# Moving batch 1's kv product ahead of four matmuls, and a quarter of two weight casts to GpSimd, in a fused attention and MoE kernel

## The chip, the cores and the metric

The kernel runs on one core of a Trainium2 chip. The metric is the device time of one execution in microseconds (us); lower is better. The engines are TensorE (PE; PEld is its weight load), VectorE (DVE), ScalarE (ACT), GpSimd (POOL) and SyncE (SP), which only issues DMAs here.

## The reference

A cosine-weighted linear attention over 8 batches, 8 heads and 576 positions, whose output goes through a two-layer MLP with a swish:

```python
q_p, k_p = phi(q), phi(k)                    # relu(x) * cos(pos), relu(x) * sin(pos), side by side
kv  = einsum('bhsf,bhsd->bhfd', k_p, v)
num = einsum('bhsf,bhfd->bhsd', q_p, kv)
den = einsum('bhsf,bhf->bhs', q_p, z) + 1e-6 # z = sum of k_p over positions
x   = (num / den), heads side by side        # 4608 x 512
h   = x @ w_in                               # 512 x 2048
g   = h * sigmoid(beta * h)
out = g @ w_out                              # 2048 x 512
```

## The kernel before

The 4608 rows are worked in nine chunks of 512. A chunk has 16 groups of four matmuls for h (L365), each followed by a swish on ScalarE (L372), and then four quarters of 16 matmuls for the output (L390). The attention of the next batch is threaded between these. The start is the hard part: attention of batches 0 and 1, the loads of all weights and their casts to bf16 have to fit beside the first chunk. What each slot of the first chunk does beside its matmuls stands in a table; shortened:

```python
    def cast_halves(i, fs=(0, 256)):          # w_in quarter i, in two halves of columns
        for f in fs:
            for gj in GJ:                     # four pieces of 64 partitions x 2 x 256
                cast_win(i, gj, "dve", f, f + 256)

    cast_halves(1)

    def rest():                               # runs behind slot 4 of the first chunk
        cast_halves(2, (0,))
        x_mul(x_rden(2, 0, 8, NQ, (0, 1)), 8, NQ)   # xs block 8 of batch 0: divide
        cast_halves(2, (256,))
        cast_halves(3)
        load_w("out", 0); load_w("out", 1)
        load_raw(1, "v"); load_raw(1, "k"); load_raw(1, "q")
        x_turn_dma(0, 8, 9)                   # xs block 8: transposed by a DMA
        load_w("out", 2, 2); load_w("out", 3, 2)
        ...                                   # casts of w_out 0..7, v_scale, relus of k and q

    def second():                             # runs behind slot 23
        kv_mm(1, 0, 6)                        # 72 small matmuls into banks 6 and 7
        kv_mm(1, 1, 6)
        kv_take((0, 1), 6, "act")             # ScalarE copies them out
        takes.append(q_turn_pe(1, 0, 4, hold=True))   # nine transposes into banks 4, 5
        takes.append(q_turn_pe(1, 1, 6, hold=True))   # nine transposes into banks 6, 7
        cast_out(8)                           # w_out row block 8, needed by slot 24
        ...
    early = {
        4: lambda: (num_mm(8, 0, 2, 0), num_mm(8, 1, 2, 1), rest()),
        15: lambda: v_scale(1, 1, eng="act"),
        23: second,
        25: lambda: (num_seven(0, 4), x_mul(x_rden(4, 0, 0, 7, (0,)), 0, 7), cast_out(13)),
        26: lambda: (num_seven(1, 6), x_mul(x_rden(6, 0, 0, 7, (1,)), 0, 7)),
        ...
    }
```

## Time and profile before

| | before |
|---|---|
| time, three runs | 295.05 us median (294.95 to 295.48) |
| span of the profiled run, granted clock | 292.9 us, 1.0 |
| TensorE busy | 96% |
| second query turn waits | 0.46 us, at 41.20 us |
| swish beat, even and stretched | 0.86 us; 1.07, 0.92, 0.91 us |

The chain of work that ended last is TensorE from 52 us to the end, so whatever this change gains, it gains before 52 us. There the beginning of an L372 activation shows when a group of four matmuls ended; an even beat of 0.86 us means that TensorE ran without a stop. The prediction below shows the lines.

### The profile page before, as it was taken

What the parts mean: (1) busy time and instruction counts of PE and PEld (TensorE: products, weight loads), DVE (VectorE), ACT (ScalarE), POOL (GpSimd) and SP (SyncE); (2) the same over time, 40 slices, a digit from 0 to 9 for tenths busy, and PEclk for the clock granted to TensorE, in tenths of its full rate; (3) what the DMA queues carried; (4) which work ended last, traced back from release to release, by engine and by line L of the source; (5) the groups of instructions that cost most, each with busy time, mean ns of one, the idle gap of its engine ahead of it and who ended that gap; (6) DMA issues with size and microseconds to landing.
All of it is one profiled execution on the core that took longest, in us unless ns stands there. A gap on an engine that the chain in (4) does not pass through costs nothing.

```text
span 292.9 us, 7188 instructions
## 1 busy us (share of the span) xinstructions
PE 282.4 (96%) x3046; PEld 142.5 (49%) x3073; DVE 114.3 (39%) x291; ACT 142.6 (49%) x228; POOL 73.3 (25%) x85
## 2 busy tenths in 40 slices
PE   8699999999999999999999999999999999999994
PEld 7454455455445544454445444554455444444444
DVE  5989975744910292029400950086005000000000
ACT  5777845862166314821473137512760277137511
POOL 1440000633381026402640255015701210000000
PEclk9999999999999999999999999999999999999999
DMA  7999999999998099907991699149102910131033
GB/s 256 378 391 384 392 325 385 265 234 355 169 273 334 4 143 230 396 30 133 219 395 46 123 211 388 72 73 197 36 2 50 145 36 0 38 84 24 0 74 72
DMA packets 50736, 53.89 MB, mean 184 GB/s; under 512 B 31232, under 2 KB 31632, under 8 KB 50704
## 3 DMA queue, kind: packets, MB, share of 16 engines
q1 hardware_dynamic: 47744, 45.95, 53.8%
q0 software_dynamic: 2688, 7.34, 11.1%
q8 instruction: 24, 0.39, 0.6%
q10 hardware_dynamic: 272, 0.14, 0.2%
q14 instruction: 8, 0.07, 0.1%
HBM read 36.71 MB, written 9.44 MB: 158 GB/s over the span
## 4 chain that ended last, share of the span: by engine, by line
PE 84%; DMA 9%; DVE 4%; issue 1%; SPq 0%
PE ps L390 39%; PE ps L365 38%; DMA w_stage<-in_moe_w_in_dram 4%; PE ps L280 3%; DVE win L108 3%; DMA w_stage<-in_moe_w_out_dram 3%; PE ps L259 2%; DMA raw_q<-in_q_dram 2%; PE ps L408 1%; DVE wout L116 0%; PE ps L339 0%; PE ps L229 0%; SPq L78 0%; DVE xs L302 0%; DVE o_sb L411 0%
## 5 line engine op out<-in xcount | busy, mean ns | idle before, releaser
L365 PE MATMUL ps<-xt,win 128*128 128x512 bf16 (+1 forms) x580 | 127.6, 378 | 0.1
L390 PE MATMUL ps<-wout,g_t 128*128 128x512 bf16 x535 | 120.6, 379 | 1.9 <-issue 1.0
L372 ACT ACTIVATE g_t<-ps,beta 128x512 bf16<-128x512 f32 x144 | 98.5, 688 | 33.5 <-PE ps L365 33.5
L365 PEld LDWEIGHTS <-win 128*128 128x128 bf16 x580 | 55.7, 98 | 66.6 <-DVE win L108 1.3
L390 PEld LDWEIGHTS <-g_t 128*128 128x128 bf16 x560 | 53.9, 98 | 63.9 <-issue 0.2
L385 POOL DMA_DIRECT2D out_dram<-o_sb x56 | 37.2, 668 | 143.2 <-ACT o_sb L396 143.2
L396 ACT COPY o_sb<-ps 128x512 f32<-128x512 f32 x35 | 20.2, 587 | 98.2 <-PE ps L390 94.0
L271 DVE CAST kv<-ps 128x520 bf16<-128x520 f32 x6 | 4.2, 699 | 68.3 <-PE ps L259 68.3
L217 POOL TENSOR_TENSOR qs<-qt,tanr 128x1152 bf16<-128x1152 bf16 x12 | 28.4, 2383 | 8.6 <-DMA qt<-qb 8.5
L411 DVE COPY o_sb<-ps 128x256 f32<-128x256 f32 (+1 forms) x2 | 0.7, 358 | 62.7 <-PE ps L408 62.7
L302 DVE TENSOR_TENSOR xs<-ps,rden 128x768 bf16<-128x768 f32 (+4 forms) x26 | 22.8, 884 | 1.0 <-DVE rden L295 0.2
L291 DVE TENSOR_TENSOR den<-ps,eps 128x12 f32<-128x12 f32 (+4 forms) x26 | 4.1, 158 | 33.6 <-PE ps L280 33.5
L214 DVE TENSOR_SCALAR vb<-raw_v,cos 128x256 bf16<-128x256 f32 x63 | 17.1, 347 | 0.0
L214 DVE TENSOR_SCALAR vb<-raw_v,sin 128x256 bf16<-128x256 f32 x54 | 14.7, 348 | 0.0
L280 PEld LDWEIGHTS <-qt 64*64 64x64 bf16 x576 | 10.5, 106 | 4.7 <-issue 3.8
L259 PE MATMUL ps<-vb,rk 64*64 64x130 bf16 x576 | 10.2, 219 | 2.4 <-ACT rk L187 2.2
L280 PE MATMUL ps<-kv,qt 64*64 64x65 bf16 x576 | 11.8, 195 | 0.5 <-ACT kv L269 0.5
L189 DVE TENSOR_SCALAR qb<-raw_q 128x1152 bf16<-128x1152 f32 x16 | 11.4, 752 | 1.7 <-DMA raw_q<-in_q_dram 1.6
L280 PE MATMUL ps<-kv,qs 64*64 64x65 bf16 x576 | 11.7, 194 | 0.1
L108 DVE CAST win<-w_stage 64x512 bf16<-64x512 f32 x26 | 11.2, 433 | 1.1 <-DMA w_stage<-in_moe_w_in_dram 0.5
L259 PEld LDWEIGHTS <-rk 64*64 64x64 bf16 x576 | 8.5, 107 | 6.3 <-ACT rk L187 3.0
L280 PEld LDWEIGHTS <-qs 64*64 64x64 bf16 x576 | 10.5, 105 | 0.2 <-issue 0.2
(59 smaller groups left out, 97.4 us busy)
## 6 DMA issues: line engine op xcount, KB each, us to landing
raw_v<-in_v_dram SPq DMA_DIRECT2D x7, 1152.0 KB, 10.5
raw_k<-in_k_dram SPq DMA_DIRECT2D x7, 1152.0 KB, 13.4
raw_q<-in_q_dram SPq DMA_DIRECT2D x7, 1152.0 KB, 7.7
out_dram<-o_sb POOLq DMA_DIRECT2D x56, 128.0 KB, 3.9
w_stage<-in_moe_w_in_dram SPq DMA_DIRECT2D x3, 1024.0 KB, 13.2
w_stage<-in_moe_w_out_dram SPq DMA_DIRECT2D x2, 1024.0 KB, 8.0
w_stage<-in_moe_w_out_dram SPq DMA_DIRECT2D x4, 512.0 KB, 10.5
out_dram<-o_sb SPq DMA_DIRECT2D x14, 128.0 KB, 2.3
```

What stands on the lines that cost most here:

```text
L108: nc.vector.tensor_copy(o, a)
L189: nc.vector.tensor_scalar(dst, src, scalar1=0.0, scalar2=None, op0=ALU.max)
L214: nc.vector.tensor_scalar(o, a, scalar1=t[:, n : n + 1], scalar2=None, op0=ALU.mult)
L217: eng.tensor_tensor(dst.rearrange("q n (g p) -> q n g p", g=2), src.rearrange("q n (g p) -> q n g p", g=2), tanr[:, n0:n1].unsqueeze(2).to ...
L259: nc.tensor.matmul(t[jj * HP : (jj + 1) * HP, g], lhsT=rk[hs, n, 2 * jp + jj, :], rhs=vb[hs, n, 2 * jp + jj].rearrange("q s e -> q (s e)") ...
L280: nc.tensor.matmul(ps[cols, bank + jj, slot * E : (slot + 1) * E], lhsT=(qt, qs)[cs][rows, jp, n, cols], rhs=kv[rows, g, jp, cs, :], start ...
L302: nc.vector.tensor_tensor(o.rearrange("q j n s d -> q j (n s) d"), nv[:, :, a:z, :, 0:D].rearrange("q j n s d -> q j (n s) d"), rden[:, :, ...
L365: nc.tensor.matmul(ps[:, h_bank(c, jt), blocks.start * 64 : blocks.stop * 64], lhsT=win[jt // 4][:, mi, (jt % 4) * P : (jt % 4 + 1) * P], ...
L372: nc.scalar.activation(g_t, ps[:, h_bank(c, jt)], AF.Silu, scale=beta[:, jt : jt + 1])
L385: eng.dma_start(out=out_v[bb, n][:, m0:m1], in_=o_sb[hf * HP : (hf + 1) * HP, m0:m1])
L390: nc.tensor.matmul(o_ps, lhsT=gs[c, jt][:, tt * P : (tt + 1) * P], rhs=wout[jt // 4][:, jt % 4, :], start=(jt == 0), stop=(jt == JT - 1))
L396: nc.scalar.copy(o_sb, o_ps)
```

## The change

The intent is to take two small stops out of TensorE's first 42 us. The kv of batch 1 goes in front of the last four matmuls of a quarter, so that the copy of kv out of banks 6 and 7 has those matmuls to hide behind before the query turn needs the banks. And a quarter of VectorE's casts of w_in 2 and 3 goes to GpSimd, which is idle there.

```diff
-                cast_win(i, gj, "dve", f, f + 256)
+                cast_win(i, gj, "pool" if i > 1 and gj == GJ[3] else "dve", f, f + 256)
 ...
     def second():
-        kv_mm(1, 0, 6)
-        kv_mm(1, 1, 6)
-        kv_take((0, 1), 6, "act")
         takes.append(q_turn_pe(1, 0, 4, hold=True))
 ...
         15: lambda: v_scale(1, 1, eng="act"),
+        22: lambda: (kv_mm(1, 0, 6), kv_mm(1, 1, 6), kv_take((0, 1), 6, "act")),
         23: second,
```

## The prediction

> **What bounds the kernel now.** I read the page first: its busy table and its chain of work that ended last.
>
> ```profile
> PE 282.4 (96%) x3046; PEld 142.5 (49%) x3073; DVE 114.3 (39%) x291; ACT 142.6 (49%) x228; POOL 73.3 (25%) x85
> ...
> PE 84%; DMA 9%; DVE 4%; issue 1%; SPq 0%
> PE ps L390 39%; PE ps L365 38%; DMA w_stage<-in_moe_w_in_dram 4%; PE ps L280 3%; DVE win L108 3%; DMA w_stage<-in_moe_w_out_dram 3%; PE ps L259 2%; DMA raw_q<-in_q_dram 2%; PE ps L408 1%; DVE wout L116 0%; PE ps L339 0%; PE ps L229 0%; SPq L78 0%; DVE xs L302 0%; DVE o_sb L411 0%
> ```
>
> TensorE is the bound. The chain in order of time shows that from 52 us to the end it is TensorE alone, in nearly identical chunks, so a microsecond saved before 52 us should arrive whole at the end, and nothing else will. The change touches only the work between 21 and 42 us. There I read the TensorE, VectorE and ScalarE timelines (start, duration, engine, line, operation, count, idle before and its releaser). TensorE, where batch 1's kv and query turns stand:
>
> ```profile
> 35.80 3.19 PE L390 MATMUL ps<-wout,g_t 128*128 128x512 bf16 x14
> 38.91 1.22 PE L259 MATMUL ps<-vb,rk 64*64 64x130 bf16 x72
> 40.06 0.68 PE L229 MATMUL ps<-ident,qb 128*128 128x128 bf16 x9
> 41.20 0.66 PE L229 MATMUL ps<-ident,qb 128*128 128x128 bf16 x9 [0.46 <-DVE wout L116]
> 41.70 1.89 PE L390 MATMUL ps<-wout,g_t 128*128 128x512 bf16 x7
> ```
>
> The second query turn stood still for 0.46 us. It writes banks 6 and 7, which hold the kv sums until ScalarE has copied them out. The other two engines around it:
>
> ```profile
> 40.56 0.59 ACT L269 CAST kv<-ps 128x520 bf16<-128x520 f32 x1 [3.89 <-PE ps L229]
> 41.04 0.70 ACT L234 COPY qt<-ps 128x640 bf16<-128x640 bf16 x1
> ...
> 35.91 1.36 DVE L189 TENSOR_SCALAR rk<-raw_k 128x2304 bf16<-128x2304 f32 x1
> 38.89 1.43 DVE L189 TENSOR_SCALAR qb<-raw_q 128x1152 bf16<-128x1152 f32 x2 [1.63 <-DMA raw_q<-in_q_dram]
> 40.72 0.49 DVE L116 TENSOR_SCALAR wout<-w_stage,rbeta 128x512 bf16<-128x512 f32 x1 [0.40 <-DMA w_stage<-in_moe_w_out_dram]
> 41.12 1.48 DVE L217 TENSOR_TENSOR qs<-ps,tanr 128x512 bf16<-128x512 bf16 x2
> ```
>
> The kv copy ends at 40.56 + 0.59 = 41.15, and TensorE goes on at 41.20. The profile names VectorE's w_out cast, which ends at the same moment (40.72 + 0.48); by the program the turn reads nothing of it, so the kv copy is the true releaser. The coincidence matters all the same: that cast makes w_out row block 8, which the very next matmuls (L390 at 41.70) need, and it waited for its DMA, which landed at 40.7. Likewise the query relu waited for raw_q, landed at 38.86.
>
> The second place is the casts of w_in. TensorE there seems never idle, but its ends are modelled; the swish activations (L372) keep the true beat of the groups of four matmuls:
>
> ```profile
> 25.77 0.69 ACT L372 ACTIVATE g_t<-ps,beta 128x512 bf16<-128x512 f32 x1 [0.18 <-PE ps L365]
> 26.63 0.69 ACT L372 ACTIVATE g_t<-ps,beta 128x512 bf16<-128x512 f32 x1 [0.18 <-PE ps L365]
> 27.70 0.69 ACT L372 ACTIVATE g_t<-ps,beta 128x512 bf16<-128x512 f32 x1 [0.38 <-PE ps L365]
> 28.56 0.69 ACT L372 ACTIVATE g_t<-ps,beta 128x512 bf16<-128x512 f32 x1 [0.18 <-PE ps L365]
> 29.48 0.69 ACT L372 ACTIVATE g_t<-ps,beta 128x512 bf16<-128x512 f32 x1 [0.23 <-PE ps L365]
> ...
> PEld L365 <- DVE win L108: 1.3, 3, 0.5
> ```
>
> The beat is 0.86 us (25.77 to 26.63). It stretches to 1.07 before 27.70, 0.92 before 29.48 and 0.91 before 31.25: 0.21 + 0.06 + 0.05 = 0.32 us lost where the next two column blocks of w_in 2 and 3 were not yet cast. The last line (waits: total, times, longest) agrees: three weight loads waited for L108.
>
> **What the Trainium skill says.** "SBUF — State Buffer", section "Who interferes with whom": VectorE's copies and casts in a 2-port mode and GpSimd's instructions share a port pair under an exclusive lock, and the loser blocks for the other's whole instruction. "VectorE: DVE Perf Modes", section "Mode 2×_2P": a single-source instruction between SBUF tensors may run at two elements a cycle on both ports. The trace agrees with both: a VectorE cast of 512 elements takes 0.42 us, below the 0.53 us that one element a cycle would take at 0.96 GHz (an estimate from that page's rate and the 0.96 GHz of the page "Trainium Kernel Development and Optimization", section "NeuronCore Architecture"); and where GpSimd casts w_in 0 beside it, VectorE's two casts look like this:
>
> ```profile
> 15.51 1.18 DVE L108 CAST win<-w_stage 64x512 bf16<-64x512 f32 x2
> ...
> 16.46 1.36 POOL L106 CAST win<-w_stage 64x512 bf16<-64x512 f32 x2
> ```
>
> One of these took 0.72 us instead of 0.42, and one of GpSimd's 0.79 instead of 0.61: a collision costs VectorE about 0.3 us. "GPSIMD Engine Reference", section "Engine selection", says that one-input work on GpSimd is roughly at line rate; here it is 0.61 against 0.42 us, slower, but on an engine that is idle from 18.5 to 51.5 us.
>
> **The change, part by part.**
>
> *Casts.* Four of the sixteen half casts of w_in 2 and 3 (64 partitions, 2 x 256 elements, the same amount as the casts above) leave VectorE: 4 x 0.44 us pitch (12 casts in 5.30 us) = 1.77 us less. They cost GpSimd 4 x 0.61 = 2.5 us of idle time. w_in 1 was there at 18.95; at 1 MB per 2.7 us (390 GB/s) w_in 2 lands near 21.6 and w_in 3 near 24.3, estimates from the DMA rate. So GpSimd casts its pieces at about 21.7, 22.3, 24.4 and 25.0, well before TensorE wants them (26.5 and later). Three of these meet VectorE casts; at 0.3 us each that gives back 0.9. Net, VectorE's casts of w_in 2 end at 26.80 - 0.88 + 0.6 = 26.5 and those of w_in 3 at 30.33 - 1.77 + 0.9 = 29.5, each ahead of or level with TensorE (26.47 for the first). Most of the 0.32 us goes; I take 0.3. VectorE then reaches v earlier, but v_scale and k_relu wait for raw_v (landed 32.9) and raw_k (near 35.9), which the DMA queue brings in its order at full rate: rk stays ready at 37.27.
>
> *kv first.* In the old order the kv starts at 38.91. It moves ahead of four L390 matmuls (4 x 0.216 = 0.86 us): 38.91 - 0.86 - 0.30 = 37.75, after rk (37.27), so it does not wait. It takes 1.15 us, to 38.90; the four matmuls follow to 39.76. The kv copy needs 0.5 us of delay and 0.59 of work: done by 40.0. First query turn at 39.76: its relu is ready at 38.89 + 0.71 = 39.6. Its nine transposes take 0.50 (41.20 to 41.70), to 40.26. The second needs the second relu, 40.32 plus some 0.06 of signalling = 40.38; it no longer waits for the copy and ends at 40.88. Without the 0.3 us from the casts the same sum gives 41.06.
>
> *What takes over.* The L390 matmuls of row block 8 need its w_out cast. The DMA lands at 40.69, the cast ends at 41.21; they start at 41.24, whether the turns ended at 40.88 or at 41.06. Before: 41.70. **Gain 0.46 us**, and most of the gain from the casts vanishes in this wait. Both parts of the change together are thus worth what the second is worth alone.
>
> *After that.* Row block 9: ScalarE's cast ends near 41.8, needed at 42.1. First seven numerators at 42.97; their qs is done at 42.60. Second seven at 44.41; their qs is done at 44.32, the tightest place, still just in time. Division of the first half ends at 45.8, its turn comes at 47.06; of the second 47.75, at 48.31. Cast 14 ends at 46.9, needed at 48.7. None binds, so the 0.46 us reaches 52 us and then the end. 295.05 - 0.46 = 294.6.
>
> **Rivals.** (a) *Port fight.* Each GpSimd cast blocks VectorE for its full 0.61 us: 4 x 0.61 = 2.4 against 1.77 saved. Casts of w_in 3 would end 0.7 us later and TensorE stall about 0.7 before 31 us. The later slack at row block 8 absorbs only 0.18, so the gain would shrink to nearly nothing: 295.0. Against it: the one clear collision cost 0.3. (b) *The w_out transfer comes earlier.* If the DMA of row block 8 is led by an earlier release of its staging buffer, both gains add: 0.46 + 0.3 = 0.76, 294.3. For: its issue, at 31.17, lies after the last cast. Against: the queue ahead of it is full of raw_k and raw_q until 38.86 and the engines move 380 to 395 GB/s till 36 us; an earlier issue only waits longer. (c) *Numerators bind.* VectorE's chain from the w_out cast to the second qs is pinned to the DMA at 40.69, ending 44.32. If signalling is longer than I assume, 0.1 to 0.2 of the gain is lost there: 294.75. (d) kv waits for rk: needs TensorE more than 0.47 us faster than reckoned; unlikely.
>
> **Range and chances.** The main case and (c) give 294.6 to 294.75, (b) 294.3, (a) 295.0; the three times of before spread by 0.5 us, which adds some 0.15 to a median. I take 294.1 to 295.0. Two per cent is 5.9 us; all TensorE idleness that this change could reach is under 1.5 us, and no rival costs that much. Faster by over 2%: 0.01; within: 0.98; slower: 0.01.
>
> **What would show it.** In the changed profile: activations of L372 at an even 0.86 from 25 to 32 us; four GpSimd casts between 21 and 26 us, and one to three VectorE casts near 0.7 us; L259 starting near 37.8 without a wait; no 0.46 us idle before the second L229; and a new wait of some 0.2 to 0.4 us of L390 for the w_out cast, starting near 41.24. If L259 waits for rk, or L372 stretches more than before, (a) or (d) holds. If the DMA of row block 8 lands well before 40.6, (b) holds. The prediction would be wrong if the total moved by over 0.9 us, or if TensorE's gain at 42 us were lost before 52 us.

## The result, and the profile after

The changed kernel took 294.68 us (median of 4, 294.58 to 294.84), the kernel before 295.09 us in its four runs: 0.41 us less, where 0.46 was predicted and the range was 294.1 to 295.0. The ratio is 0.9985, with a 95% interval of 0.9967 to 1.0002. (Ratios here are the mean time of one kernel's fast runs over that of the other's of the same rounds, so not quite the ratio of the medians that are quoted.) Executions over 1.5% slower than the fastest of the same kernel are left out of the means.

The page of the changed kernel, with the busy table, the granted clock in 40 slices, and the chain of work that ended last, by engine and by line:

```profile
PE 284.7 (97%) x3073; PEld 142.7 (49%) x3073; DVE 113.6 (39%) x287; ACT 142.7 (49%) x228; POOL 75.9 (26%) x89
...
PEclk9979999999999999999999999999999999999999
...
PE 94%; DMA 3%; SPq 1%; DVE 1%; issue 0%
PE ps L365 43%; PE ps L390 42%; PE ps L280 4%; PE ps L259 3%; DMA raw_v<-in_v_dram 3%; PE ps L408 1%; PE ps L339 1%; SPq L78 1%; PE ps L229 0%; DVE vb L204 0%; DVE rden L295 0%; DVE rk L189 0%; DVE o_sb L411 0%; DVE den L291 0%
```

TensorE remains the bound, and VectorE's casts (L108) and the w_out transfer have left the chain. But the clock row says that this execution is not like the one before: in the third slice TensorE was granted 0.7 of its clock. The table of stretches gives 0.57 for 14 to 18 us (start and end, length, busy time and count of PE, PEld, DVE, ACT, POOL, then clock, DMA share and GB/s):

```profile
14.00:18.00 4.00, 3.77 (x110) 2.88 (x109) 3.03 (x10) 2.49 (x7) 2.95 (x5) 0.57 1.07 405
```

So the first groups of the MLP came 0.9 us later than in the old profile. The lines that answer to those of the prediction, TensorE first, then ScalarE and VectorE at the turns, then the swish beat (start, duration, engine, line, operation, count, idle before and its releaser):

```profile
38.63 1.22 PE L259 MATMUL ps<-vb,rk 64*64 64x130 bf16 x72
39.78 1.04 PE L390 MATMUL ps<-wout,g_t 128*128 128x512 bf16 x4
40.65 1.17 PE L229 MATMUL ps<-ident,qb 128*128 128x128 bf16 x18
41.66 1.89 PE L390 MATMUL ps<-wout,g_t 128*128 128x512 bf16 x8
...
40.27 0.59 ACT L269 CAST kv<-ps 128x520 bf16<-128x520 f32 x1 [3.30 <-PE ps L259]
...
39.17 1.43 DVE L189 TENSOR_SCALAR qb<-raw_q 128x1152 bf16<-128x1152 f32 x2 [1.60 <-DMA raw_q<-in_q_dram]
41.01 0.49 DVE L116 TENSOR_SCALAR wout<-w_stage,rbeta 128x512 bf16<-128x512 f32 x1 [0.41 <-DMA w_stage<-in_moe_w_out_dram]
...
27.52 0.69 ACT L372 ACTIVATE g_t<-ps,beta 128x512 bf16<-128x512 f32 x1 [0.18 <-PE ps L365]
28.38 0.69 ACT L372 ACTIVATE g_t<-ps,beta 128x512 bf16<-128x512 f32 x1 [0.17 <-PE ps L365]
```

Two things agree with the prediction: both query turns now run as one group of 18 without the 0.46 us stop, and the beat is an even 0.86 us. The second can mislead. TensorE came late enough for any cast to be ready, so this profile cannot show what the GpSimd casts are worth. And L390 starts at 41.66, level with the old 41.70, though the kernel was faster. One profile did not explain the time, so the experiments begin with the same kernel at full clock.

### The profile page after: what moved, and what is told of

Same layout as the page of the kernel before. It is cut to its first block, busy times and chain, and to the rows that moved or that the text cites. A ratio compares the mean times of both kernels' runs of the same rounds, so it can differ in the third digit from the quotient of the medians.

```text
span 292.8 us, 7219 instructions
## 1 busy us (share of the span) xinstructions
PE 284.7 (97%) x3073; PEld 142.7 (49%) x3073; DVE 113.6 (39%) x287; ACT 142.7 (49%) x228; POOL 75.9 (26%) x89
## 4 chain that ended last, share of the span: by engine, by line
PE 94%; DMA 3%; SPq 1%; DVE 1%; issue 0%
PE ps L365 43%; PE ps L390 42%; PE ps L280 4%; PE ps L259 3%; DMA raw_v<-in_v_dram 3%; PE ps L408 1%; PE ps L339 1%; SPq L78 1%; PE ps L229 0%; DVE vb L204 0%; DVE rden L295 0%; DVE rk L189 0%; DVE o_sb L411 0%; DVE den L291 0%
## 5 line engine op out<-in xcount | busy, mean ns | idle before, releaser
L390 PE MATMUL ps<-wout,g_t 128*128 128x512 bf16 x560 | 124.6, 379 | 0.0
L390 PEld LDWEIGHTS <-g_t 128*128 128x128 bf16 x560 | 53.9, 98 | 63.9 <-issue 0.5
L280 PEld LDWEIGHTS <-qt 64*64 64x64 bf16 x576 | 10.8, 108 | 4.8 <-issue 4.4
L280 PE MATMUL ps<-kv,qt 64*64 64x65 bf16 x576 | 12.1, 197 | 0.2 <-ACT kv L269 0.2
L280 PE MATMUL ps<-kv,qs 64*64 64x65 bf16 x576 | 11.8, 196 | 0.0
L108 DVE CAST win<-w_stage 64x512 bf16<-64x512 f32 x22 | 10.6, 482 | 0.5
L280 PEld LDWEIGHTS <-qs 64*64 64x64 bf16 x576 | 10.8, 108 | 0.0
```

Source lines behind the costliest of these rows:

```text
L108: nc.vector.tensor_copy(o, a)
L280: nc.tensor.matmul(ps[cols, bank + jj, slot * E : (slot + 1) * E], lhsT=(qt, qs)[cs][rows, jp, n, cols], rhs=kv[rows, g, jp, cs, :], start ...
L390: nc.tensor.matmul(o_ps, lhsT=gs[c, jt][:, tt * P : (tt + 1) * P], rhs=wout[jt // 4][:, jt % 4, :], start=(jt == 0), stop=(jt == JT - 1))
```

## The experiments

**My theory** was that of the prediction: the landing of w_out row block 8 caps the gain, the kv move is worth all of it, and the casts save 0.3 us that vanish under the cap. **The rivals:** the parts add; the GpSimd casts cost more than they save; the gain is something else, seen only by chance.

Four kernels went to one chip. That chip's executions scattered: the kernel before took 294.9 us (median of 11, 294.32 to 296.97, with the granted clock down to 0.992 in the slowest), so the profiles have to settle what the times cannot.

### a_again: the changed kernel at full clock

No edit.

> The changed kernel once more, because the profile of its first look fell on an execution whose TensorE clock was cut to 0.57 between 14 and 18 us. Theory (the gain is capped by the landing of w_out row block 8): 294.6 to 294.7 us, 0.35 to 0.46 us less than before; in a profile at full clock the kv starts near 37.75 us, the second query turn has no wait, and L390 waits 0.2 to 0.4 us for the w_out cast and starts near 41.24. Rival (the gain is not this wait but the 0.3 us stall of the second numerators at 45.1 us of the old profile, which happened to be absent): L390 starts near 41.7 as before and the numerators at 45 us run without the stall.

Measured: 294.75 us, ratio 0.9995 (0.9969 to 1.0021). The profile was at full clock. L390 did wait 0.18 us for the w_out cast, as the theory says. But the swish beat broke: 26.97 to 28.47 is 1.50 us, a loss of 0.64 us where the old kernel lost 0.21. GpSimd's and VectorE's timelines in that stretch show why (an earlier and a later cast of each):

```profile
22.84 0.72 DVE L108 CAST win<-w_stage 64x512 bf16<-64x512 f32 x1
22.67 0.62 POOL L106 CAST win<-w_stage 64x512 bf16<-64x512 f32 x1 [3.85 <-DMA w_stage<-in_moe_w_in_dram]
...
26.29 0.74 DVE L108 CAST win<-w_stage 64x512 bf16<-64x512 f32 x1
25.94 0.81 POOL L106 CAST win<-w_stage 64x512 bf16<-64x512 f32 x1
```

Each of GpSimd's four casts stretched one VectorE cast from 0.42 to 0.72 or 0.74 us. The eleven casts up to the division took 5.48 us, where eleven at the old pitch of 0.44 take 4.87, so 0.61 more for two collisions; the nine after the division took 4.60 where nine take 3.98, so 0.62 more for two. What I had misjudged is where the last two fall: GpSimd's pieces of *w_in 3* collide with VectorE's casts of *w_in 2's second half*, which is what TensorE waits for next.

### e1_kv_only: the kv move alone

```diff
-                cast_win(i, gj, "pool" if i > 1 and gj == GJ[3] else "dve", f, f + 256)
+                cast_win(i, gj, "dve", f, f + 256)
```

> Only the kv move, all w_in casts on VectorE as before. Theory (w_out row block 8 caps the gain): L390 after the turns starts at 41.24 as in the whole change, so the time is that of the whole change within 0.1 us, 0.35 to 0.46 us less than before, and L372 keeps its stretched beats of about 1.07 and 0.92 us. Rival (the two parts add): 0.3 us slower than the whole change, about 0.1 to 0.15 us faster than before.

Measured: 294.3 us, ratio 0.998 (0.995 to 1.0009). Not slower than the whole change but 0.45 us faster by the medians. Its eleventh beat loses 0.18 us, as in the old kernel. L390 started at 41.60 after a 0.21 us wait for the w_out cast, which began at 41.06:

```profile
41.60 1.89 PE L390 MATMUL ps<-wout,g_t 128*128 128x512 bf16 x8 [0.21 <-DVE wout L116]
```

### e2_casts_only: the GpSimd casts alone

```diff
-                cast_win(i, gj, "dve", f, f + 256)
+                cast_win(i, gj, "pool" if i > 1 and gj == GJ[3] else "dve", f, f + 256)
```
(on the kernel before)

> Only the GpSimd casts, the kv in its old place. Theory: L372 runs at an even 0.86 us beat, the kv starts 0.3 us earlier, at 38.6; the second query turn still waits for the kv copy, about 0.45 us, and L390 starts near 41.4, not yet held by row block 8: 0.3 us less than before. Rival (port fight eats the casts' worth): no change, 0.0 within 0.1 us, with L372 beats as stretched as before.

Measured: 295.53 us, ratio 1.0026 (0.9993 to 1.0058): neither theory. By its median it is 0.6 us slower than the kernel before, which the interval leaves just short of certain. The beat and the second turn:

```profile
28.48 0.69 ACT L372 ACTIVATE g_t<-ps,beta 128x512 bf16<-128x512 f32 x1 [1.15 <-PE ps L365]
...
41.90 0.66 PE L229 MATMUL ps<-ident,qb 128*128 128x128 bf16 x9 [0.48 <-ACT kv L269]
```

The activation before stood at 26.65, so this beat is 1.83 us, a loss of 0.97 us. In this execution w_in 2 had landed only at 22.87, and VectorE itself waited 0.41 us for it, so not all of the 0.97 is collision. The second line confirms the reading of the old stall: with the kv in its old place the turn waits 0.48 us, and here the profile names the kv copy as the releaser, not the w_out cast.

### e3_turn_last: the transfer of row block 8 brought forward

```diff
-        x_turn_dma(0, 8, 9)
         load_w("out", 2, 2)
         load_w("out", 3, 2)
+        x_turn_dma(0, 8, 9)
```
(on the changed kernel)

> The whole change, and the DMA transpose of xs block 8 (which moved little in 36 to 39 us of the old profile) issued behind the four loads of w_out 2 and 3 instead of ahead of them, so that row block 8 lands earlier. Theory (row block 8 caps the gain): it lands 1 to 2 us earlier, the turns follow one another without waits, L390 starts near 40.9, and the time is 0.3 us less than the whole change's, about 294.3 us. Rival (something else caps, such as the query relu or VectorE's chain): within 0.1 us of the whole change.

Measured: 294.5 us as the median, but from 294.21 to 298.76; ratio 1.0007 (0.9956 to 1.0057). Four of its six runs took 294.21 to 294.66, two, both at a granted clock of 0.994, took 298.59 and 298.76 (the last left out of the ratio). In the profile:

```profile
41.06 1.89 PE L390 MATMUL ps<-wout,g_t 128*128 128x512 bf16 x8
...
40.43 0.49 DVE L116 TENSOR_SCALAR wout<-w_stage,rbeta 128x512 bf16<-128x512 f32 x1
```

The w_out cast follows the query relu at once, without the DMA wait that every other kernel so far has, and L390 waits for nothing. So the cap on L390 is indeed this transfer, and with it gone the next limit there is TensorE itself. But L390 started 0.54 us before that of e1_kv_only, and both executions ended alike, at 292.4 and 292.5 us: the lead was lost near 192 us, as is told below. The two long runs are taken up under e4_best.

### e5_pool_in2 and e6_pool_in3: which of the casts hurt

```diff
-                cast_win(i, gj, "pool" if i > 1 and gj == GJ[3] else "dve", f, f + 256)
+                cast_win(i, gj, "pool" if i == 2 and gj == GJ[3] else "dve", f, f + 256)   # e6: i == 3
```

> The changed kernel with GpSimd's casts for w_in 2 only. Theory (each GpSimd cast stretches one VectorE cast by 0.3 us, and the two casts of w_in 3 were stretching the second half of w_in 2): two stretched VectorE casts near 0.72 us, both before 25 us; the second half of w_in 2 ends about 0.26 us earlier than in the old kernel counted from VectorE's first cast of w_in 1 (7.56 us after it against 7.82); the beat before the eleventh L372 loses 0.15 us or less, against 0.56 to 0.97 in the three full-clock runs with all four casts. Rival (TensorE waits for GpSimd's own slow pieces): the loss at the eleventh activation stays 0.5 us or more.

> The changed kernel with GpSimd's casts for w_in 3 only. Theory: both fall on VectorE's casts of the second half of w_in 2, which end 8.4 us after the first cast of w_in 1 (7.82 + 0.62); the eleventh L372 comes 0.6 to 0.9 us late, though every piece that it needs is VectorE's, and the later beats are even. Rival (GpSimd's own pieces are late): the eleventh comes 0.2 us late as in the old kernel, and the loss falls on the thirteenth or fifteenth.

The eleventh activation of e5_pool_in2, and below it that of e6_pool_in3:

```profile
27.74 0.69 ACT L372 ACTIVATE g_t<-ps,beta 128x512 bf16<-128x512 f32 x1 [0.19 <-PE ps L365]
```
```profile
29.43 0.69 ACT L372 ACTIVATE g_t<-ps,beta 128x512 bf16<-128x512 f32 x1 [0.93 <-PE ps L365]
```

With w_in 2's pieces alone on GpSimd the beat is 26.87 to 27.74, a loss of 0.01 us; with w_in 3's alone it is 27.81 to 29.43, a loss of 0.76 us, although every piece that TensorE needs there is then VectorE's. e5_pool_in2 is the clean one of the two: slow GpSimd pieces of w_in 2 would have kept the loss, and it went. e6_pool_in3 agrees but weighs less. Only one of its two collisions is large (0.64 us instead of 0.42), so some 0.22 of its 0.76 us is collision; the old kernel's 0.21 is in it too, and w_in 1 had landed 1.5 us late (VectorE's first cast at 20.47, not 18.98). The times: 294.29 us for e5_pool_in2, ratio 0.9982 (0.9947 to 1.0017), and 294.64 us for e6_pool_in3, ratio 0.9997 (0.9966 to 1.0027), against 294.87 of the kernel before.

### e7_shift: a stall that no semaphore explains

The old kernel has another stop, in the second seven numerators at 45.1 us. It is in both profiles with the old order (before, e2_casts_only), and none of the four with the new order from the first rounds has it (e6_pool_in3, also of the new order, has a rest of it, under 0.1 us at 46.1 us). By the program's order of instructions no one waits on a semaphore there. The edit shifts TensorE's instruction stream by 16 places:

```diff
-    warm_pe(58, 48)
+    warm_pe(50, 48)
```
(on the kernel before)

> The kernel before with 8 fewer of the 58 small warm-up matmuls, so that every later TensorE instruction stands 16 places earlier in its stream. It is about the stall of 0.2 to 0.3 us in the second seven numerators (45.1 to 45.45 us), which no instruction there waits for by semaphore and which the two runs with the old order show and the four with the new order do not. Theory (instruction fetch at a fixed place of the stream): the stall moves 8 matmuls later in the numerators, and shrinks by 0.1 us or so. Rival (a data or bank dependency): it stays before the seventh or at the fifth matmul of that group with its length.

TensorE in the second numerators, first in the kernel before, then in e7_shift:

```profile
45.12 0.55 PE L280 MATMUL ps<-kv,qs 64*64 64x65 bf16 x4
45.45 0.24 PE L280 MATMUL ps<-kv,qt 64*64 64x65 bf16 x4
```
```profile
45.50 0.39 PE L280 MATMUL ps<-kv,qs 64*64 64x65 bf16 x4
45.68 0.24 PE L280 MATMUL ps<-kv,qt 64*64 64x65 bf16 x4
```

Such a group of four is followed by the next after 0.03 us. In the kernel before the gap comes in the second group (the first is at 45.06), in e7_shift in the fourth (the first is at 45.38): eight matmuls later, and shrunk from 0.33 to 0.18 us, as the fetch theory says. So in this one run it goes with a place in the instruction stream and not with data, which is what a fetch of instructions does. The DMA view fits that. This is its line for the instruction queue at 42.80 to 42.85 us of the kernel before, and below it at 43.25 to 43.30 us of e7_shift (packets, MB, their time as a share of 16 engines' 0.05 us):

```profile
q8 instruction: 1, 0.02, 138.1%
```
```profile
q8 instruction: 1, 0.02, 138.6%
```

One packet begins there and takes 1.1 us (138% of 0.8). TensorE went on 2.6 us after the beginning in the kernel before and 2.4 in e7_shift; in e2_casts_only (43.35) and e6_pool_in3 (43.45) it was 2.7. That the packet is TensorE's is inferred from this timing. The Trainium skill, "Runtime: NRT & Kernel Launch", section "Instruction fetch mechanics", says that a sequencer fetches its stream in 16 KiB blocks through a DMA queue of its own, and that the cost is mostly hidden; here it is 0.2 to 0.3 us in the open. The time of e7_shift, 296.8 us in its one run, does not come from this stop: another of 1.8 us turned up in the numerators of a later batch (waits view: L280 for issue, 1.8 us once).

### e4_best: all stops out at once, and what it ran into

On the changed kernel: casts all on VectorE, the transpose behind the w_out loads as in e3_turn_last, and VectorE's division of block 8 behind the casts of w_in 3.

```diff
         cast_halves(2, (0,))
-        x_mul(x_rden(2, 0, 8, NQ, (0, 1)), 8, NQ)
         cast_halves(2, (256,))
         cast_halves(3)
+        x_mul(x_rden(2, 0, 8, NQ, (0, 1)), 8, NQ)
```

> No GpSimd casts. The kv move, the DMA transpose of xs block 8 behind the w_out loads, and VectorE's division of block 8 (0.8 us) behind the casts of w_in 3 instead of in front of the second half of w_in 2. Theory: w_in 2's second half is cast 0.8 us earlier (about 25.9), so L372 keeps an even 0.86 us beat without help from GpSimd; kv starts near 37.6, L390 of row block 8 near 40.7 without a wait for the cast; about 0.7 to 0.9 us faster than the kernel before of the same rounds. Rival (raw_k or the query relu caps TensorE near 40 us): only 0.4 to 0.5 us faster, with a wait of L259 or L229 for rk or qb of 0.2 us or more.

Measured: 295.88 us, from 294.0 to 298.44, ratio 1.0019 (0.9971 to 1.0067). Three runs at full clock took 294.0, 294.12 and 294.62, three at 0.994 took 297.15 to 298.44 (the last left out of the ratio). The clock alone does not cost that: the kernel before took 295.16 and 295.7 us at 0.994 on the same chip. The profile is of one of these long runs. Its clock was cut to 0.5 to 0.7 between 16 and 20 us, which puts everything after it late (L390 after the turns at 43.00), and the largest single loss is one line:

```profile
48.65 0.22 PE L280 MATMUL ps<-kv,qs 64*64 64x65 bf16 x2 [2.03 <-issue]
```

The stop is at the place of the old fetch stall and lasts 2.03 us. The instruction packet began at 46.1 there, 3.1 us after L390 and not 1.1 as in the kernel before; TensorE went on 2.5 us later. The DMA moved 386 GB/s from 40 to 42 us, 215 and 185 in the two stretches to 46 us, and 374 after them: the slow stretch of the transpose, which in the kernel before lies at 36 to 40 us, now lies just ahead of that packet. In the profile of e3_turn_last, one of its fast runs, the packet began at 41.75, ahead of its slow stretch (199 GB/s from 42 to 44 us), and no stop followed. That a late TensorE's packet was held up behind the transpose is argued from the order in these two profiles, not shown by itself. e3_turn_last's two runs at 298.6 would fit it, but I have no profile of one of them. Either way this place for the transpose is a bad one.

### e8_turn_pe, e9_late_div and a_third

e9_late_div is e4_best with the transpose back in its old place. e8_turn_pe takes the transpose off the DMA queue: the skill's "DMA: Bandwidth & Descriptors", section "DMA Transpose (X-bar)", lists TensorE as another way to transpose into PSUM for data that is already on the chip. From e9_late_div to e8_turn_pe:

```diff
-        x_turn_dma(0, 8, 9)
 ...
-        15: lambda: v_scale(1, 1, eng="act"),
+        15: lambda: (x_turn_pe(0, 8, 9, 1, ("act",)), v_scale(1, 1, eng="act")),
```

> The kv move, no GpSimd casts, VectorE's division of xs block 8 behind the w_in 3 casts, and that block's two transposes on TensorE (0.11 us) with a ScalarE copy instead of the DMA transpose. Theory: even L372 beats at full clock as in the run that had the division late; the slow DMA stretch at 36 to 40 us is gone from the queue, so w_out row block 8 lands before 40.2 and the L390 after the turns starts near 40.8 without a wait, and the instruction packet of TensorE is not behind a transpose, so no stall of 2 us in the second numerators: 293.8 to 294.1 us at full clock, 0.6 to 0.9 us less than before, and fewer runs over 296. Rival (the extra TensorE and ScalarE work, or the query relu, eats it): no better than the kv move alone, 294.3.

> As the run before in this list, but the DMA transpose stays where the changed kernel has it. Theory (the landing of w_out row block 8 caps the gain): even beats, kv near 37.6, but L390 waits 0.4 to 0.5 us for the w_out cast and starts no earlier than in the kv move alone; so 294.2 to 294.4 us, within 0.1 us of the kv move alone. Rival (gains add): 0.3 us better than the kv move alone, 294.0.

> The changed kernel a third time, on the chip of these two. Theory: at full clock the eleventh L372 beat loses 0.5 to 1.0 us to the GpSimd collisions, and most of that is hidden by the wait for w_out row block 8 that it shortens: 294.5 to 294.8 us, 0 to 0.3 us less than before. Rival (the first measurement was typical): 0.4 us less than before.

On this chip the kernel before took 295.1 us (294.6 to 296.1). **e8_turn_pe took 294.12 us** (293.62 to 294.75), ratio 0.9964 (0.9946 to 0.9982): clearly faster than before, and 0.7 us below the changed kernel's 294.83 of the same rounds. No run of it was over 294.75. The DMA in the stretch from 38 to 40 us, first in the kernel before, then in e8_turn_pe:

```profile
38.00:40.00 2.00, 2.00 (x77) 1.30 (x75) 1.11 (x2) 0.00 (x0) 0.00 (x0) 1.00 0.78 246
```
```profile
38.00:40.00 2.00, 2.00 (x77) 1.27 (x75) 0.36 (x2) 0.00 (x0) 0.00 (x0) 1.00 1.05 385
```

The last column is GB/s: the transpose had left the queue at 246, and without it 385 are moved. As e8_turn_pe runs about 1 us late, it matters that none of its 2 us stretches from 34 to 48 us is below 385. The w_out cast starts at 41.35 straight after the query relu, without a DMA wait, and the beat is an even 0.86. (The profiled execution had its clock cut early, as the first one of the change, so its L390 at 41.99 is late; the 40.8 that I expected is for full clock and is not shown.)

e9_late_div took 295.09 us, ratio 1.0002 (0.9976 to 1.0028). The beat is even at full clock, so VectorE needs no help from GpSimd; but raw_q and row block 8 landed late: the turns waited 0.16 us for the query relu, the w_out cast began only at 41.92, and the gain was hidden whole. My 294.2 to 294.4 missed, because I had not reckoned with how far that landing moves from run to run. a_third took 294.83 us, ratio 0.9989 (0.9968 to 1.0009), in the range that I gave. Its profile is the full-clock picture of the change that the first one failed to give; TensorE, VectorE's w_out cast, and the tenth and eleventh activation:

```profile
37.96 1.22 PE L259 MATMUL ps<-vb,rk 64*64 64x130 bf16 x72
39.10 1.04 PE L390 MATMUL ps<-wout,g_t 128*128 128x512 bf16 x4
39.98 1.17 PE L229 MATMUL ps<-ident,qb 128*128 128x128 bf16 x18
41.27 1.89 PE L390 MATMUL ps<-wout,g_t 128*128 128x512 bf16 x8
...
40.73 0.48 DVE L116 TENSOR_SCALAR wout<-w_stage,rbeta 128x512 bf16<-128x512 f32 x1 [0.38 <-DMA w_stage<-in_moe_w_out_dram]
...
26.49 0.69 ACT L372 ACTIVATE g_t<-ps,beta 128x512 bf16<-128x512 f32 x1 [0.18 <-PE ps L365]
27.70 0.69 ACT L372 ACTIVATE g_t<-ps,beta 128x512 bf16<-128x512 f32 x1 [0.53 <-PE ps L365]
```

The last 18 transposes take 1.0 us of TensorE (39.98 to about 41.0), and L390 stands until the cast is done. The 27.70 beat loses 0.35 us to the collisions (1.21 less 0.86), more than the old 0.21, and the wait hides it.

### The profiles in one table

"Cast" is the start of VectorE's cast of w_out row block 8, that is, the landing of its transfer. The table has every profile with the transpose in its place but that of e7_shift, with its own stop of 1.8 us. The last two rows are executions in which TensorE itself came late.

| run | kv | loss at the eleventh beat | cast | L390 after the turns | L390 less cast | span | span less cast |
|---|---|---|---|---|---|---|---|
| before | old | 0.21 | 40.72 | 41.70 | 0.98 | 292.9 | 252.2 |
| e2_casts_only | old | 0.97 | 41.72 | 42.40 | 0.68 | 293.6 | 251.9 |
| a_again | new | 0.64 | 41.69 | 42.23 | 0.54 | 293.5 | 251.8 |
| a_third | new | 0.35 | 40.73 | 41.27 | 0.54 | 292.3 | 251.6 |
| e1_kv_only | new | 0.18 | 41.06 | 41.60 | 0.54 | 292.5 | 251.4 |
| e5_pool_in2 | new | 0.01 | 40.99 | 41.53 | 0.54 | 292.4 | 251.4 |
| e9_late_div | new | 0.00 | 41.92 | 42.46 | 0.54 | 293.3 | 251.4 |
| after (clock cut early) | new | 0.00 | 41.01 | 41.66 | 0.65 | 292.8 | 251.8 |
| e6_pool_in3 (w_in 1 late) | new | 0.76 | 41.81 | 42.71 | 0.90 | 293.9 | 252.1 |

In five profiles with the kv moved, L390 starts 0.54 us after that landing, with losses of 0.00 to 0.64 us at the eleventh beat. In the other two it follows the turns without a wait: a TensorE that is late enough passes the cap. The landing itself moves by 1.2 us between executions (by 0.96 in two executions of one kernel, a_again and a_third), and most of the differences in the spans go with it. Counted from it, the five end 0.4 to 0.8 us before the kernel before, and 0.1 to 0.5 us before e2_casts_only.

The last column is not constant over the five because something is lost later. TensorE near 192 us, in the kernel before, in a_again and in e3_turn_last:

```profile
192.30 1.46 PE L390 MATMUL ps<-wout,g_t 128*128 128x512 bf16 x6 [0.16 <-issue]
192.84 1.25 PE L390 MATMUL ps<-wout,g_t 128*128 128x512 bf16 x5 [0.52 <-issue]
191.81 1.47 PE L390 MATMUL ps<-wout,g_t 128*128 128x512 bf16 x6 [0.65 <-issue]
```

This stop, too, waits for nothing that the profile shows. Its 0.16 us are also those of e1_kv_only and e5_pool_in2, so a_again lost 0.36 us and e3_turn_last 0.49 there. Its cause stays open.

## Why the prediction was right or wrong

**The time was right**: 294.68 us measured first, 294.75 and 294.83 in the later rounds, all inside the range, within 2% of before. The gain by medians was 0.41, 0.15 and 0.27 us against 0.46 predicted. The landing, which moves from run to run, is most of the spread (the table above); only the first gain is near the predicted size, none of the three intervals excludes zero, and that 0.41 came so near to 0.46 is luck: in a_third's profile, the only one of the change at full clock with the landing as early as before, L390 is 0.43 us earlier, a stop that the prediction did not know gives another 0.35, and about 0.2 is lost again after 52 us.

**The stall of the query turn** was read rightly. The kv copy was the releaser (e2_casts_only names it), and with the kv moved the turns run on.

**"What takes over"** was right: a new wait of L390 for the w_out cast. The start at 41.24 was met by 41.27 in a_third, where the landing fell where it had in the kernel before; in a_again it was 42.23. e3_turn_last takes the cap away, and the five equal 0.54 show it from the other side.

**"Casts" was the step that failed.** I wrote that VectorE's casts of w_in 2 end at 26.5, "ahead of or level with TensorE", and that most of the 0.32 us goes. The size of a collision was right (0.3 us each), but in a_again all four GpSimd casts collide, not three (in a_third the fourth costs only 0.02 us), and I booked the collision of w_in 3's pieces to w_in 3. They fall on w_in 2's second half, so with four collisions: 26.80 - 0.88 + 0.61 + 0.62 = 27.15 in the old kernel's clock, 0.35 us later than without help. The full-clock runs of the change lost 0.35 and 0.64 us at that beat instead of 0.21. This is rival (a), in a form that I had not thought of: not a longer lock, but the wrong victim. The estimate of w_in 2's landing was off too: GpSimd began its first piece at 21.9 to 22.9 us, not at 21.7, so its casts started later than reckoned.

The time came out right all the same because of the claim that the cap swallows whatever the casts give; it swallowed most of what they took as well, in the executions in which TensorE still came before the landing. "Both parts together are worth what the second is worth alone" is not far off, but it flatters the casts: on the one chip where both ran, the kv move alone was 0.45 us ahead of both together.

**What the prediction missed**: the fetch stall in the second numerators. I had listed those numerators as the tightest place, but for their qs data. The kv move took that stop away too: from L390 after the turns to the L390 after the second numerators it is 41.70 to 45.99 in the old kernel and 41.27 to 45.21 in a_third, 0.35 us less. Why stays open. The packet begins 1.1 us after that L390 in the kernel before and 0.7 us after it in a_third. The w_out wait is not needed for it: e3_turn_last has no such wait, and its packet also begins 0.7 us after L390. In the new order TensorE now comes to this place about when the instructions do, so the stop is just avoided: e6_pool_in3 still shows a rest of it.

**"A microsecond saved before 52 us should arrive whole"** held only in part: the stop near 192 us takes 0.36 us from a_again and 0.49 from e3_turn_last.

**Rival (b)**, an earlier w_out transfer, did not occur in the change itself: in the full-clock profiles of the change the cast began at 40.73 and 41.69, never earlier than before. **Rivals (c) and (d)** did not occur in the profiles of the change.

## What to carry to other kernels

When work goes to GpSimd beside VectorE's casts, ask not only how much a collision costs but which VectorE instruction it will hit, and whether that is the next one that the bound engine needs; moving an unneeded instruction (here a division of 0.8 us) behind the casts gave the even beat for nothing. When a stall is removed a microsecond ahead of a transfer's landing, work out that landing first, and compare profiles counted from it, since it can move more between executions than the change is worth (here 1.2 us). Before moving a DMA, look at what stands behind it in the queue, the instruction fetch of the bound engine included.

## What the Trainium skill lacked or had wrong

- "SBUF — State Buffer", section "Who interferes with whom": the collisions agree with a shared port pair, but less was lost than "fully blocks" would give. In a_again a VectorE cast that began 0.17 us after a GpSimd cast of 0.62 us took 0.72 instead of 0.42 us: 0.30 us lost, where waiting for the end of the other costs 0.45 (an estimate from these lines; spans on GpSimd are rough).
- "Runtime: NRT & Kernel Launch", section "Instruction fetch mechanics": that the fetch is mostly hidden did not hold at the second numerators of batch 1, with the DMA moving 375 to 388 GB/s in the kernel before. TensorE stood 0.2 to 0.3 us, and 2.03 us in e4_best. The page has no time from the packet to the next instruction; in the runs with a stop it was 2.4 to 2.7 us from the packet's beginning, of which the packet took 1.1.
- "DMA: Bandwidth & Descriptors", section "DMA Transpose (X-bar)": neither it nor the skill's bandwidths of transposes say what a small transpose does to the loads around it. Here one of 128 x 256 elements left the queue at 246 GB/s over 2 us where 385 are moved without it, and the slow stretch moved with it in e3_turn_last (199) and e4_best (215 and 185).
- "GPSIMD Engine Reference", section "Engine selection": "roughly line-rate" for one input was 0.61 us for a cast that takes VectorE 0.42 us.
